# Stationary operands of 48 instead of 64 columns in the state products of a linear-attention and feed-forward kernel

## The chip, the cores and the metric

The kernel runs on one core of a Trainium2 chip. The metric is the device time of one execution in microseconds (us); lower is better. The engines are named as in the profile: PE is the matrix engine (PEld its weight loads, which overlap the products), DVE the vector engine, ACT the scalar engine, POOL the GpSimd engine, SP the queue that issues the DMA transfers.

## The reference, cut to what matters

```python
for t in range(S):                       # B, H, S, D = 4, 8, 768, 48
    kt, vt, rt = k[:, :, t], v[:, :, t], r[:, :, t]
    cur = einsum('bhd,bhe->bhde', u[None] * kt, vt)
    y[:, :, t] = einsum('bhd,bhde->bhe', rt, state + cur)
    state = w[None, :, :, None] * state + einsum('bhd,bhe->bhde', kt, vt)
x = y.transpose(0, 2, 1, 3).reshape(B * S, H * D)      # 3072 x 384
h = x @ w_in                                            # 384 x 2048
g = where(h > 0, h, exp(min(h, 0)) - 1)
out = g @ w_out                                         # 2048 x 384
```

## The kernel before, in words

The 768 tokens of a batch are cut into six blocks of 128 (n = 0 to 5). A pair of a block and one of the four batches is called a unit here, (n, b). The attention part works on units; the feed-forward part works on a whole block of four units, in 16 steps f = 0 to 15, one for each 128 columns of the hidden layer. A step holds nine wide products into `ps_h` (`hidden`, L1202), the activation, and nine wide products into `ps_acc` (`project`, L1258, of an earlier step). Beside the feed-forward steps of block n run the attention units of block n + 1, one unit for four steps. So units (1, b) run beside steps of block 0, and the later ones beside blocks 1 to 4. Beside block 0 the feed-forward weights are also made ready: each step, DVE joins words in `merge` and `sign` (L592, L600, into `wide`), ACT casts them in `split_w` (L620, into `wh`), and POOL takes the rest in `rest_w` (L630, into `wl`).

The engines take their instructions in the order in which the program issues them. That order is written out by hand: the string `FIRST` for steps of block 0 and `LATER` for the others. A word such as `ss9` names an operation and, in its last digit, the stage of a unit at which it is issued (8 is the unit's base step, 9 the step after it). In both strings the words of a step follow one another in program order, so a word that is moved is moved on the queue of its own engine.

A unit goes like this. `A` (`scores_halves`) computes the score products (L925) and behind them, in `added_halves` (L939), the products k by v that are added to the state, one for each head and each half of the block's 128 tokens: 16 products in a unit, 8 in units of the last block. Each counts as two weight loads and two matmuls in the trace. Their stationary operand is `k[HALVES[s], h, :]`, the head's 48 channels and 16 columns of padding, 64 columns; two heads share the 128 partitions of the result, which lies in the same PSUM banks as the scores. `pa` and `pb` (`take_halves`, L987, DVE) take the masked scores. `ss` (`sum_states`, DVE) adds the first half's products to the state, giving `mid` (L949), and the second half's to `mid`, giving `sw` (L952). `Y` (`outputs_halves`, L1003 and L1011) multiplies by the state, `mid` and the scores. `sw` (`next_state`, calling `decay_added`, L955, POOL) multiplies the tile `sw` by the decay and writes the state. The two words of a step that close the feed-forward's own work on DVE are `elu` (L1217) and `gl` (L1225), with `gh` (L1223) on ACT between them.

Of the kernel before, what the change touches and what calls it, by code (L numbers as in the profile page):

```python
# [8 lines left out]
F32 = mybir.dt.float32  # L9
# [8 lines left out]
P = 128  # L18
B, H, S, D = 4, 8, 768, 48
DP = 64  # L20
HP = H // 2
# [3 lines left out]
NCH = S // P  # L25
# [3 lines left out]
ROWS = [slice(i * DP, i * DP + D) for i in range(2)]  # L29
HALVES = [slice(i * DP, (i + 1) * DP) for i in range(2)]  # L30
# [18 lines left out]

FIRST = """  # L50

D9 lb ma ru4 hid wd Ya A9 neg rud8 t5 mb xya xaa sp elu ss9 kr8 kr4 pb9 bk7 rkb pa9 sum8 xha sum7 gh Lw xlda T8 dr8 gl br7 r3 r4 D7 m6 tka8 Gb swb vb proj
"""
LATER = """

A8 pb8 ss8 br7 rk9 hid pa8 neg rud4 kr4 xy9 Y8 elu t4 sw8 xa9 v9 bk6 gh gl xh9 xl9 G9 m4 proj D6 sum5
"""


class Kernel:  # L60
# [336 lines left out]
    def step(self, n, f):  # L397
        nc = self.nc

        k = f + 2 if n == 0 else NF + 1  # L400
        units = self.stages(n, f)


        last = divmod(n * NF + f - (1 if (n, f) < EARLY else 2), NF)
        both = {
            "ru": lambda n, b: self.current(n, b),
            "rud": lambda n, b: self.current(n, b, nc.vector),
            "sum": lambda n, b: self.current_sum(n, b),
            "kr": lambda n, b: self.key_rest(n, b),
            "krd": lambda n, b: self.key_rest(n, b, nc.vector),  # L410
            "D": lambda n, b: self.diag_halves(n, b),
            "A": lambda n, b: self.scores_halves(n, b),
            "pa": lambda n, b: self.take_halves(n, b, 0),
            "pb": lambda n, b: self.take_halves(n, b, 1),
            "ss": lambda n, b: self.sum_states(n, b),
            "Y": lambda n, b: self.outputs_halves(n, b),
            "xy": lambda n, b: self.take_outputs(n, b),
            "xa": lambda n, b: self.add_outputs(n, b),
            "sw": lambda n, b: self.next_state(n, b),
            "rk": lambda n, b: self.load_after(n, b, self.load_rk),  # L420
            "v": lambda n, b: self.load_after(n, b, self.load_v),
            "xh": lambda n, b: self.split_added(n, b, 0),
            "xl": lambda n, b: self.split_added(n, b, 1),
            "xld": lambda n, b: self.split_added(n, b, 1, nc.vector),
            "xhp": lambda n, b: self.split_added(n, b, 0, nc.gpsimd),
            "xhd": lambda n, b: self.split_added(n, b, 0, nc.vector),
            "xyd": lambda n, b: self.take_outputs(n, b, nc.vector.tensor_copy),
            "G": lambda n, b: self.fill_x(n, b),
        }
        by_pe = {  # L430
            "T": lambda n, b: self.turn_in(n, b),
            "dr": lambda n, b: self.decay_r(n, b),
            "dk": lambda n, b: self.decay_k(n, b),
            "tk": lambda n, b: self.take_k(n, b, nc.vector.tensor_copy),
            "tka": lambda n, b: self.take_k(n, b, nc.scalar.copy),
        }
        moved = {
            "t": lambda n, b: self.turn_blocks(n, b),
            "m": lambda n, b: self.move_blocks(n, b),
            "br": lambda n, b: self.decay_moved(n, b),  # L440
            "bk": lambda n, b: self.join_moved(n, b),
        }
        layer = {
            "hid": lambda: self.hidden(n, f, self.rest_of(n, f)),
            "ma": lambda: self.merge(k),
            "mb": lambda: self.sign(k),
            "neg": lambda: self.negative(n, f),
            "sp": lambda: self.split_w(k),
            "spd": lambda: self.split_w(k, nc.vector.tensor_copy),
            "r4": lambda: self.rest_w(k, 1),  # L450
            "r3": lambda: self.rest_w(k, 0),
            "r4d": lambda: self.rest_w(k, 1, nc.vector),
            "r3d": lambda: self.rest_w(k, 0, nc.vector),
            "elu": lambda: self.elu(n, f),
            "gh": lambda: self.split_g(n, f, 0),
            "gl": lambda: self.split_g(n, f, 1),
            "proj": lambda: self.project(*last) if last in self.g else None,
            "Lw": lambda: [self.load_weights(j) for j in (2 * k + 2 * DEEP - 1, 2 * k + 2 * DEEP) if n == 0],
            "wd": lambda: self.widen(k + 1),
            "lb": lambda: self.low_bits(k + 1),  # L460
        }
        for op in (LATER if n else FIRST).split():
            if op in layer:
                layer[op]()
                continue
            name, stage = op[:-1], int(op[-1], 16)
            for at, m, b in units:
                todo = {**both, **(by_pe if m == 1 else moved)}
                key = self.KINDS.get(name, name), m, b
                if at == stage and name in todo and key not in self.done:  # L470
                    self.done.add(key)
                    todo[name](m, b)
        if last[1] == NF - 1 and last[0] in self.acc:
            self.store(last[0])
        self.store_pending(2)
        if (n, f) == (0, NF - 1):

            o = self.late.bitcast(F32).rearrange("p s d w -> p (s d w)")[:, 0 : B * DM]
            self.o = o.rearrange("p (b d) -> p b d", b=B)
# [451 lines left out]
    def added_halves(self, n, b, banks):  # L931
        nc, un = self.nc, self.units[n, b]
        k, v = self.raw[n, b][1], self.v_of(n, b)
        un["kv"] = [t[:, 2 * P : 2 * P + HP * D] for t in banks]
        for a in range(HP):
            for i in range(2):
                for s in range(1 if n + 1 == NCH else 2):
                    h = 2 * a + i
                    nc.tensor.matmul(  # L939
                        un["kv"][s][HALVES[i], a * D : (a + 1) * D],  # L940
                        lhsT=k[HALVES[s], h, :], rhs=v[HALVES[s], h, :],
                        start=True, stop=True, skip_group_check=True,
                    )

    def sum_states(self, n, b):
        nc, un = self.nc, self.units[n, b]
        kv = [t.rearrange("p (a c) -> p a c", a=HP) for t in un["kv"]]
        mid = self.mid[:, :, 0:D]
        nc.vector.tensor_add(mid, self.state[b][:, :, 0:D], kv[0])  # L949
        if n + 1 < NCH:  # L950
            un["sw"] = self.wk.tile([P, HP, D], F32, tag="sw", name="sw", bufs=1)
            nc.vector.tensor_add(un["sw"], mid, kv[1])  # L952

    def decay_added(self, b, t):
        self.nc.gpsimd.tensor_mul(  # L955
            self.state[b][:, :, 0:D], t, self.pw[:, :, P : P + 1].to_broadcast([P, HP, D])
        )

    def next_state(self, n, b):
        if n + 1 < NCH:  # L960
            self.decay_added(b, self.units[n, b]["sw"])

    def first_state(self, b):
        nc = self.nc
# [373 lines left out]
```

## Time and profile before

| what | us |
|---|---|
| time, median of 3 runs | 491.83 (491.37 to 492.10) |
| span of the profiled execution, first to last instruction | 490.3 |
| around the span (median less span) | 1.5 |
| PE busy in the span | 479.5 (98%) |
| weight loads busy | 396.6 (81%) |
| DVE busy | 286.2 (58%) |
| ACT busy | 253.4 (52%) |
| POOL busy | 151.6 (31%) |

The profile comes from one execution, of which the span is what is recorded; the time of a run holds some 1.5 us more than it. Busy times are sums over stages that differ: beside block 0 (about 37 to 105 us from the start of the span) all four engines are nearly full, and later PE alone is.

### The profile page before, as it was taken

How to read it: one execution, taken by the hardware profiler on the slowest of the kernel's cores; microseconds unless marked ns; L12 is line 12 of the kernel's file. 1: busy time of each engine (PE TensorE's matmuls, PEld its weight loads, DVE VectorE, ACT ScalarE, POOL GpSimd, SP SyncE). 2: the span in 40 equal slices, each digit the busy share in tenths (PEclk: the TensorE clock that was granted, in tenths of full speed). 3: DMA queues.
4: the chain of work that ended last, by engine and by line, in shares of the span. 5: the costliest groups of instructions: out<-in, count | busy, mean ns of one | idle time of the engine just before them, and what ended most of it. 6: DMA issues, size and time to landing. Idle time of an engine off the chain costs nothing.

```text
span 490.3 us, 11493 instructions
## 1 busy us (share of the span) xinstructions
PE 479.5 (98%) x4640; PEld 396.6 (81%) x4640; DVE 286.2 (58%) x507; ACT 253.4 (52%) x453; POOL 151.6 (31%) x169
## 2 busy tenths in 40 slices
PE   8989999999999999999999999999999999999995
PEld 6788877878788888788888888888888888899994
DVE  8989999987555545745455565364554433433332
ACT  3469898864463443453553544544534535444442
POOL 5376769672241331241232223213203201000000
PEclk9999999999999999999999999999999999999999
DMA  7985866652543451443541623623524400020002
GB/s 160 227 202 172 195 181 191 158 130 70 124 128 84 117 138 43 122 123 73 141 114 38 153 86 84 157 59 96 146 58 123 108 13 11 18 48 0 1 0 71
DMA packets 109955, 51.04 MB, mean 104 GB/s; under 512 B 89027, under 2 KB 105797, under 8 KB 109893
## 3 DMA queue, kind: packets, MB, share of 16 engines
q1 hardware_dynamic: 109892, 50.22, 40.8%
q8 instruction: 38, 0.62, 0.6%
q14 instruction: 25, 0.20, 0.1%
HBM read 35.13 MB, written 13.11 MB: 98 GB/s over the span
## 4 chain that ended last, share of the span: by engine, by line
PE 81%; DVE 6%; POOL 3%; DMA 3%; SPq 2%; ACT 2%; issue 1%; DVEq 0%; ACTq 0%; POOLq 0%
PE ps_h L1202 36%; PE ps_acc L1258 29%; PE ps_acc L1245 7%; PE ps_y L1003 2%; DMA k_t<-in_k_dram 2%; PE ps_a L925 2%; POOL wl L630 2%; DVE wide L600 2%; DVE wide L592 2%; PE ps_y L1011 2%; PE ps_a L939 2%; DMA stage<-in_moe_w_out_dram 1%; SPq L205 1%; PE ps_y L873 1%; ACT wh L620 1%
## 5 line engine op out<-in xcount | busy, mean ns | idle before, releaser
L1202 PE MATMUL ps_h<-x,wh 128*128 128x512 f32 (+1 forms) x588 | 176.2, 389 | 0.0
L1258 PE MATMUL ps_acc<-g,wh 128*128 128x512 f32 x480 | 164.0, 396 | 0.0
L1217 DVE SCALAR_TENSOR_TENSOR ps_h<-g,ps_h 128x512 f32<-128x512 f32 x96 | 66.6, 693 | 145.5 <-ACT g L1212 145.5
L1211 ACT ACTIVATE g<-ps_h 128x512 f32<-128x512 f32 x96 | 57.3, 597 | 150.1 <-PE ps_h L1202 150.0
L1202 PEld LDWEIGHTS ps_h<-x,wh 128*128 128x128 f32 x588 | 108.2, 188 | 21.4
L1202 PE MATMUL ps_h<-x,wl 128*128 128x512 f32 (+1 forms) x294 | 109.0, 387 | 0.3
L1258 PEld LDWEIGHTS ps_acc<-g,wh 128*128 128x128 f32 x480 | 90.1, 188 | 20.2 <-DVE stage L1266 0.5
L1258 PE MATMUL ps_acc<-g,wl 128*128 128x512 f32 x240 | 93.6, 390 | 0.0
L1225 DVE TENSOR_TENSOR g<-ps_h,g 128x512 fp32r<-128x512 f32 x96 | 65.7, 685 | 42.6 <-ACT g L1223 40.6
L1223 ACT CAST g<-ps_h 128x512 fp32r<-128x512 f32 x96 | 56.2, 585 | 43.4 <-DVE ps_h L1217 43.2
L1202 PEld LDWEIGHTS ps_h<-x,wl 128*128 128x128 f32 x294 | 55.0, 188 | 12.6 <-POOL wl L630 1.6
L1212 ACT ACTIVATE g<-g 128x512 f32<-128x512 f32 x96 | 60.7, 632 | 3.1
L1040 POOL TENSOR_TENSOR x<-x_f,x 128x512 fp32r<-128x512 f32 x16 | 20.7, 1292 | 116.3 <-ACT x L1038 116.3
L753 POOL TENSOR_TENSOR k_t<-k_t,rev 128x384 f32<-128x384 f32 x21 | 23.7, 1133 | 100.6 <-DVE ru L735 100.4
L1258 PEld LDWEIGHTS ps_acc<-g,wl 128*128 128x128 f32 x240 | 45.1, 188 | 8.4
L630 POOL TENSOR_TENSOR wl<-wide,wh 128x384 fp32r<-128x384 f32 x29 | 33.8, 1190 | 15.9 <-ACT wh L620 15.9
L1245 PE MATMUL ps_acc<-wh,g 128*128 128x384 f32 x128 | 35.1, 337 | 0.0
L980 POOL TENSOR_TENSOR a<-ident_h,diag 128x512 f32<-128x512 f32 x20 | 23.7, 1185 | 2.5 <-PE ps_a L925 2.5
L1245 PEld LDWEIGHTS ps_acc<-wh,g 128*128 128x128 f32 x128 | 23.4, 188 | 0.6
L600 DVE SCALAR_TENSOR_TENSOR wide<-stage,wide 128x768 int32<-128x768 int32 (+1 forms) x17 | 21.3, 1256 | 0.5
L1245 PE MATMUL ps_acc<-wl,g 128*128 128x384 f32 x64 | 21.5, 336 | 0.0
L674 POOL TENSOR_TENSOR rk<-rk,pw 128x512 f32<-128x512 f32 x16 | 19.0, 1190 | 5.7 <-DMA rk<-blocks 5.7
(128 smaller groups left out, 460.3 us busy)
## 6 DMA issues: line engine op xcount, KB each, us to landing
blocks<-tb SPq DMA_DIRECT2D x64, 128.0 KB
rk<-blocks SPq DMA_DIRECT2D x16, 512.0 KB
stage<-in_moe_w_out_dram SPq DMA_DIRECT2D x16, 384.0 KB
stage<-in_moe_w_in_dram SPq DMA_DIRECT2D x32, 144.0 KB
r_t<-in_r_dram SPq DMA_DIRECT2D x22, 192.0 KB
k_t<-in_k_dram SPq DMA_DIRECT2D x22, 192.0 KB
v_t<-in_v_dram SPq DMA_DIRECT2D x22, 192.0 KB
out_dram<-stage SPq DMA_DIRECT2D x80, 48.0 KB
```

The source lines that it names most:

```text
L600: self.nc.vector.scalar_tensor_tensor(a, high, -(2**31), a, op0=ALU.bitwise_and, op1=ALU.bitwise_or)
L630: (eng or self.nc.gpsimd).tensor_sub(lo, a, hi.bitcast(F32))
L753: (eng or self.nc.gpsimd).tensor_mul(k, k, self.rev[:, :, 0:D])
L980: self.nc.gpsimd.tensor_mul(un["a"], self.ident_h.unsqueeze(1).to_broadcast([P, H, DP]), un["diag"].unsqueeze(2).to_broadcast([P, H, DP]),)
L1202: self.nc.tensor.matmul(ph[:, part], lhsT=a[:, c * P : (c + 1) * P], rhs=x[:, c, part], start=(i == 0), stop=(i + 1 == len(todo)),)
L1211: nc.scalar.activation(g, ph, AF.Relu, scale=-1.0)
L1212: nc.scalar.activation(g, g, AF.Exp, scale=-1.0)
L1217: self.nc.vector.scalar_tensor_tensor(ph, g, -1.0, ph, op0=ALU.add, op1=ALU.max)
L1223: nc.scalar.copy(part, g)
L1225: nc.vector.tensor_sub(part, g, self.g[n, f][2].bitcast(F32))
L1245: self.nc.tensor.matmul(self.acc[n][b][:, 0:DM], lhsT=a[:, at], rhs=w, start=(f == 0 and i == 0), stop=(f == NF - 1 and i == 2),)
L1258: self.nc.tensor.matmul(self.acc[n][c], lhsT=w[:, c * P : (c + 1) * P], rhs=g, start=(f == 0 and i == 0), stop=(f == NF - 1 and i == 2),)
```

## The change

In `added_halves` the stationary operand loses its padding: `k[HALVES[s], h, 0:D]`, 48 columns, and the result lies on `ROWS[i]`, partitions 0 to 47 and 64 to 111, instead of all 128. Since 16 partitions between the two ranges are no longer written, everything that read the sums in one instruction over 128 partitions now goes by two ranges of 48. `sum_states` writes only `mid`, in two instructions. What made `sw` is now a part of its own. Beside block 0 it is `se` (`sum_ends`): two DVE additions. Later it is `ta` (`take_ends`), two ACT copies out of PSUM, and `ad` (`add_ends`), two POOL additions of `mid`. `next_state` calls `decay_rows`, two POOL multiplications. In `FIRST`, `ss9` moves from behind `elu` to ahead of it and `se9` comes behind `pb9`; in `LATER`, `ta8 ad8` come behind `pa8`, ahead of `neg`.

```diff
-... sp elu ss9 kr8 kr4 pb9 bk7 rkb pa9 ...            (FIRST)
+... sp ss9 elu kr8 kr4 pb9 se9 bk7 rkb pa9 ...
-A8 pb8 ss8 br7 rk9 hid pa8 neg rud4 ...                (LATER)
+A8 pb8 ss8 br7 rk9 hid pa8 ta8 ad8 neg rud4 ...
...
-                        un["kv"][s][HALVES[i], a * D : (a + 1) * D],
-                        lhsT=k[HALVES[s], h, :], rhs=v[HALVES[s], h, :],
+                        un["kv"][s][ROWS[i], a * D : (a + 1) * D],
+                        lhsT=k[HALVES[s], h, 0:D], rhs=v[HALVES[s], h, :],
...
     def sum_states(self, n, b):
+        un = self.units[n, b]
+        for rows in ROWS:
+            kv = un["kv"][0][rows].rearrange("p (a c) -> p a c", a=HP)
+            self.nc.vector.tensor_add(self.mid[rows, :, 0:D], self.state[b][rows, :, 0:D], kv)
+
+    def sum_ends(self, n, b):
...
+        for rows in ROWS:
+            kv = un["kv"][1][rows].rearrange("p (a c) -> p a c", a=HP)
+            self.nc.vector.tensor_add(un["sw"][rows], self.mid[rows, :, 0:D], kv)
+
+    def take_ends(self, n, b):
...
+        for rows in ROWS:
+            kv = un["kv"][1][rows].rearrange("p (a c) -> p a c", a=HP)
+            self.nc.scalar.copy(un["sw"][rows], kv)
+
+    def add_ends(self, n, b):
...
+        for rows in ROWS:
+            self.nc.gpsimd.tensor_add(un["sw"][rows], un["sw"][rows], self.mid[rows, :, 0:D])
...
+    def decay_rows(self, b, t):
+        for rows in ROWS:
+            self.nc.gpsimd.tensor_mul(
+                self.state[b][rows, :, 0:D], t[rows],
+                self.pw[rows, :, P : P + 1].to_broadcast([D, HP, D]),
+            )
 
     def next_state(self, n, b):
         if n + 1 < NCH:
-            self.decay_added(b, self.units[n, b]["sw"])
+            self.decay_rows(b, self.units[n, b]["sw"])
```

## Rows read from the trace of the kernel before

**Rows 1.** Two stretches: us, then busy us (instructions) of PE, PEld, DVE, ACT, POOL.
```profile
77.00:97.00 20.00, 19.85 (x208) 15.86 (x207) 18.52 (x26) 17.83 (x33) 15.96 (x13) 1.00 0.62 172
200.00:300.00 100.00, 100.00 (x1033) 81.05 (x1034) 53.17 (x102) 46.81 (x86) 26.29 (x27) 1.00 0.43 107
```

**Rows 2.** The chain that ended last, 92 to 140 us: start, us, what.
```profile
96.04 1.19 POOL state L955
...
101.02 2.67 POOL wl L630 x2
...
103.74 0.96 PE ps_h L1202 x3
...
113.44 2.27 PE ps_h L1202 x9
```

**Rows 3.** DVE in order of time, 78.5 to 88.5 us: start, duration, what.
```profile
79.79 1.67 DVE L600 SCALAR_TENSOR_TENSOR wide<-stage,wide 128x768 int32<-128x768 int32 x1
81.38 0.68 DVE L1217 SCALAR_TENSOR_TENSOR ps_h<-g,ps_h 128x512 f32<-128x512 f32 x1
81.98 0.34 DVE L949 TENSOR_TENSOR mid<-state,ps_a 128x192 f32<-128x192 f32 x1
82.45 0.35 DVE L952 TENSOR_TENSOR sw<-mid,ps_a 128x192 f32<-128x192 f32 x1
82.72 0.77 DVE L987 COPY_PREDICATED a<-mask,ps_a 128x256 f32<-128x256 int32 x2
83.39 0.68 DVE L1225 TENSOR_TENSOR g<-ps_h,g 128x512 fp32r<-128x512 f32 x1
83.99 1.13 DVE L592 SCALAR_TENSOR_TENSOR wide<-stage 128x768 int32<-128x768 int32 x1
85.15 1.65 DVE L600 SCALAR_TENSOR_TENSOR wide<-stage,wide 128x768 int32<-128x768 int32 x1
```

**Rows 4.** ACT in order of time, 78.5 to 88.5 us, with idle time ahead.
```profile
81.50 0.93 ACT L620 CAST wh<-wide 128x384 fp32r<-128x384 f32 x2 [0.26 <-DVE wide L600]
82.33 0.58 ACT L1223 CAST g<-ps_h 128x512 fp32r<-128x512 f32 x1
...
86.83 0.93 ACT L620 CAST wh<-wide 128x384 fp32r<-128x384 f32 x2 [0.62 <-DVE wide L600]
```

**Rows 5.** Weight loads in order of time, at 23 to 26 and at 262 us.
```profile
23.63 0.55 PEld L968 LDWEIGHTS ps_st<-raw 128*64 128x64 f32 x16
24.73 0.97 PEld L776 LDWEIGHTS ps_a<-rk 48*128 48x128 f32 x16 [0.55 <-DVE x L894]
...
262.35 0.56 PEld L939 LDWEIGHTS ps_a<-v_t,k_t 64*64 64x64 f32 x32
```

**Rows 6.** Groups of instructions over the whole span: busy us, mean ns of one load.
```profile
L939 PEld LDWEIGHTS ps_a<-v_t,k_t 64*64 64x64 f32 x576 | 11.2, 135 | 0.0
...
L776 PEld LDWEIGHTS ps_a<-rk 48*128 48x128 f32 x64 | 3.9, 187 | 1.9 <-POOL rk L696 0.8 <-DVE x L894 0.5 <-DVE rk L698 0.4
```

**Rows 7.** The instructions of line 955: count, duration min/median/max in ns.
```profile
L955 POOL TENSOR_TENSOR state<-sw,pw x16: 514/518/1227, 55.3 to 323.6; 128x192 f32<-128x192 f32 x16
```

**Rows 8.** DVE in order of time, 92 to 106 us: the transpose that waits.
```profile
101.05 0.71 DVE L651 STREAM_TRANSPOSE tb<-k_t 128x512 f32<-128x512 f32 x1 [0.30 <-POOL k_t L753]
```

**Rows 9.** DVE in order of time, 41 to 46.5 us: L600 beside an idle POOL.
```profile
44.96 0.96 DVE L600 SCALAR_TENSOR_TENSOR wide<-stage,wide 128x768 int32<-128x768 int32 x1
```

**Rows 10.** A unit beside block 2, engines in order of time, 261.9 to 275 us.
```profile
264.19 0.44 DVE L987 COPY_PREDICATED a<-mask,ps_a 128x256 f32<-128x256 int32 x1
...
267.87 0.67 DVE L651 STREAM_TRANSPOSE tb<-k_t 128x512 f32<-128x512 f32 x1
...
265.34 0.60 ACT L1211 ACTIVATE g<-ps_h 128x512 f32<-128x512 f32 x1 [2.77 <-PE ps_h L1202]
...
265.74 1.02 POOL L753 TENSOR_TENSOR k_t<-k_t,rev 128x384 f32<-128x384 f32 x1 [7.29 <-DVE ru L735]
...
265.23 0.46 PE L1003 MATMUL ps_y<-rk,state 48*64 48x64 f32 x16
```

More of the change, by code (lines that the diff above doesn't have):

```diff
@@ L50 @@
 FIRST = """
-D9 lb ma ru4 hid wd Ya A9 neg rud8 t5 mb xya xaa sp elu ss9 kr8 kr4 pb9 bk7 rkb pa9 sum8 xha sum7 gh Lw xlda T8 dr8 gl br7 r3 r4 D7 m6 tka8 Gb swb vb proj
+D9 lb ma ru4 hid wd Ya A9 neg rud8 t5 mb xya xaa sp ss9 elu kr8 kr4 pb9 se9 bk7 rkb pa9 sum8 xha sum7 gh Lw xlda T8 dr8 gl br7 r3 r4 D7 m6 tka8 Gb swb vb proj
 """
 LATER = """
-A8 pb8 ss8 br7 rk9 hid pa8 neg rud4 kr4 xy9 Y8 elu t4 sw8 xa9 v9 bk6 gh gl xh9 xl9 G9 m4 proj D6 sum5
+A8 pb8 ss8 br7 rk9 hid pa8 ta8 ad8 neg rud4 kr4 xy9 Y8 elu t4 sw8 xa9 v9 bk6 gh gl xh9 xl9 G9 m4 proj D6 sum5
 """
@@ L415, in step @@
             "ss": lambda n, b: self.sum_states(n, b),
+            "se": lambda n, b: self.sum_ends(n, b),
+            "ta": lambda n, b: self.take_ends(n, b),
+            "ad": lambda n, b: self.add_ends(n, b),
             "Y": lambda n, b: self.outputs_halves(n, b),
@@ L945, in sum_states @@
     def sum_states(self, n, b):
[L946 to L952, printed above, removed]
+        un = self.units[n, b]
[3 more added lines that the diff above has]
+    def sum_ends(self, n, b):
+        un = self.units[n, b]
+        if n + 1 == NCH:
+            return
+        un["sw"] = self.wk.tile([P, HP, D], F32, tag="sw", name="sw", bufs=1)
+        for rows in ROWS:
+            kv = un["kv"][1][rows].rearrange("p (a c) -> p a c", a=HP)
+            self.nc.vector.tensor_add(un["sw"][rows], self.mid[rows, :, 0:D], kv)
+    def take_ends(self, n, b):
+        un = self.units[n, b]
+        if n + 1 == NCH:
+            return
+        un["sw"] = self.wk.tile([P, HP, D], F32, tag="sw", name="sw", bufs=1)
+        for rows in ROWS:
+            kv = un["kv"][1][rows].rearrange("p (a c) -> p a c", a=HP)
+            self.nc.scalar.copy(un["sw"][rows], kv)
+    def add_ends(self, n, b):
+        un = self.units[n, b]
+        if n + 1 == NCH:
+            return
+        for rows in ROWS:
+            self.nc.gpsimd.tensor_add(un["sw"][rows], un["sw"][rows], self.mid[rows, :, 0:D])
     def decay_added(self, b, t):
```

## The prediction, made before the changed kernel ran

> **What bounds the kernel now.** I read the busy times by stretch first, because the change does different things in two stages. In a stretch of 100 us in the middle PE is busy all of it, DVE about half, POOL a quarter [rows 1]: there PE's own work alone sets the time, and whatever makes its products shorter comes off the end. Beside block 0 it is another picture: in 20 us, PE 19.85, DVE 18.52, ACT 17.83, POOL 15.96 [rows 1]. When four engines are that full, the question is which loop of waits sets the pace. The chain shows PE released by POOL there, at 103.74 us, by the rest of a weight (L630), with the decay of the state (L955) earlier on that chain [rows 2]. So PE is not what bounds it. Nor is POOL, if one asks what starts its rests: the casts on ACT (L620), which start when DVE's L600 ends [rows 4].
>
> The loop itself is read from DVE and ACT side by side. In a step without a unit's sums it goes L600, L620 on ACT, L1223 on ACT, then DVE again. In the step that holds them it is DVE alone: L600 at 79.79, L1217, L949, L952, two L987, L1225 at 83.39, L592, and the next L600 at 85.15, with hardly a gap [rows 3]; the ACT cast that L1225 needs ended at 82.91, 0.48 us before it was wanted, and ACT then waited 0.62 us for that next L600 [rows 4]. One such step stands here for each of the four units (1, b). An instruction put between L600 and L1225 there is on the loop.
>
> **The products.** How much does a load of 48 columns save? I saw no row of one at this clock. In L939, 32 loads take 0.56 us over four tiles of the array [rows 5]; less one load's own 0.135 [rows 6], 31 intervals, 13.7 ns each, 55 ns for a round of four. In L968, two tiles, 16 loads take 0.55 [rows 5]: 27.5 ns each, again 55 ns for a round. So the pace is a tile's, not that of issue. L776 loads 128 columns into two tiles: 0.97 [rows 5] less 0.19 [rows 6] over 15 intervals, 104 ns a round. From 64 to 128 columns a round thus grows by 0.77 ns a column; 48 would take 43, 12 ns less. The moving operand has 48 columns already, so I don't expect it to hold the round up. A unit with 16 products has eight rounds, of which the first loads under the tail of the scores: seven times 12 is 0.086 us; a last-block unit, three times, 0.037. Beside blocks 1 to 4 stand twelve of the former and four of the latter: 1.2 us off PE's saturated stretch. From below: nothing, if a load pays for the tile's 64 columns whatever is in it. From above, all rounds count: 1.35. I take 1.2, as the rounds follow the column count. In the four units (1, b) a shorter product gains nothing, as PE waits there.
>
> **The DVE additions beside block 0.** Two become four, each over the same 192 elements of a partition. I read no row with 48 partitions; half as many partitions cost as much, or some part of it down to nothing, and I take the whole, since the stream of 192 elements is what stays. From start to start, L952 to L987 is 0.27 us [rows 3], so two more add 0.55 between L600 and L1225; 0.94 if each takes the 0.47 that lies between L949 and L952. Moving the first two ahead of `elu` delays the ACT cast L1223 by about as much, which its 0.48 and the later additions on DVE hide. Behind L1225 all is late by 0.55: L592, L600, the casts, the rests on POOL, PE's next product. Four units: 2.2 us.
>
> **The POOL decay beside block 0.** One L955 becomes two; it takes 0.51 at the least and 1.23 at the most [rows 7]. Behind it on POOL are the products that prepare the next k, then the rests that PE waits for [rows 2]. For the steps of (1, 1) and (1, 2), POOL's lateness runs beside DVE's and the larger counts. Ahead of (1, 3) it adds: there DVE's transpose already waited 0.30 us for POOL's k [rows 8], so DVE gets later by what POOL gets later. I take 0.5, between nothing and 1.23: the long L955 started while an L600 of 1.65 or so ran, against 0.96 for one beside an idle POOL [rows 3, 9], and the second half comes when that is over. The Trainium skill (SBUF — State Buffer, Who interferes with whom) has a rule for this: a DVE instruction with two SBUF inputs and a GpSimd one that reads SBUF exclude each other for a whole instruction. By that rule the second half costs 0.5; by doubling the longest row 1.2, and the forecast would be 0.7 higher.
>
> **The later blocks' new work.** DVE keeps two additions. ACT gets two copies of 192 elements, at most 0.58 each by L1223 with 512 [rows 4], ahead of an activation that waits 2.77 us for PE [rows 10]: hidden; without that cover up to 1.2 a unit. POOL gets two additions and one more decay, 0.5 to 1.2 each by L955 [rows 7]. It idles 7.29 us up to L753, which has to be done only for the transpose at 267.87, 1.1 us after its end [rows 10]. Additions that get in the way of the DVE products for which L753 waits may push it by 1.0 and still fit. Next to be late would be the transfer for the following unit, not PE. The outputs on PE at 265.23 need the scores taken, which is done at 264.63 [rows 10], and now ACT's copies too, since both lie in the banks that the outputs reuse: L939's loads end at 262.91 [rows 5], two copies by 264.1. Cost: nothing.
>
> **Sum.** 2.2 and 0.5, less 1.2: 1.5 us. The profiled span of 490.3 becomes 491.8; around it the runs have 1.5 more, so 491.83 becomes 493.3, slower by 0.3%. About 0.2%, 1 us, is what a measurement of this kernel tells from no change.
>
> **Rivals.** *The loads don't shrink:* a tile of 64 columns keeps its 55 ns. Against it, rounds of 64 and 128 columns differ nearly in proportion [rows 5]. Then 491.83 + 2.7 = 494.5. *The additions are absorbed*, which ends on the other side. DVE's L592 and L600 took 1.13 and 1.65 beside POOL's rests, and L600 0.96 beside an idle POOL [rows 3, 9]. Shifted by half a microsecond against POOL, they may stop colliding: up to 0.7 back for each L600, more than the 0.55 spent. With nothing lost beside block 0 the time is 490.6; it is faster than before once block 0 costs under 1.2 us, 0.3 a unit. For it: every long L600 was one beside POOL. Against it: POOL's own queue moves too. *Half absorbed:* the collision is undone in one or two of the four steps, block 0 costs 1.2 to 1.6, and the time stays at 491.8 to 492.2. *A later unit waits:* ACT's copies, run late, hold the banks and with them the outputs; it decides once they end after 265.23 in such a unit, 1.1 us later than they can. At 0.2 us a unit over twelve units this is 2.4 more: 495.7. The 2.77 us of idle ACT speak against it.
>
> **How the numbers follow.** The sum as it stands 0.48, no smaller loads 0.12, absorbed 0.18, half absorbed 0.18, a later wait 0.04. The first stays within 0.2% in a fifth of its cases (a unit costing 0.4 instead of 0.55), so slower 0.54, same 0.28, faster 0.18. Low is 490.6, all absorbed; high 494.8, just above loads that don't shrink; the likeliest case by itself spans 492.4 to 494.3.
>
> **What would show it.** L939's 32 loads in about 0.47 instead of 0.56 us, and a unit's period beside block 2 shorter by 0.09. Beside block 0, four additions where two were, and from L600 to L600 in that step 5.9 instead of 5.36; L955 as pairs with a second half near 0.5; PE's first wide product of block 1, now at 113.44 [rows 2], later by 2.7. The prediction is wrong if that product is not at least 1.5 us late, if L939 keeps 0.56, or if PE shows gaps ahead of the outputs from block 1 on.

## The result, and the profile after

The changed kernel takes 495.11 us (median of 4 runs, 494.8 to 496.3); the kernel before, on the same chip, 491.78 (4 runs, 491.37 to 492.1). The ratio is 1.007, 95% interval 1.0057 to 1.0082: slower by 3.3 us, where the forecast was slower by 1.5, in a range that ended at 494.8. The profiled execution has a span of 494.6 us and is the run of 496.3; its mean granted clock was 0.993. The other three runs had 0.996 to 0.999 and took 494.8 to 495.35. The changed kernel was run a second time as an experiment (e11, below), and that profile, with a clock of 0.999, is the cleaner one for sums.

The later blocks first, since there the forecast held. These are the stretches of [rows 1], the columns as there.

```profile
77.00:97.00 20.00, 18.97 (x205) 15.15 (x204) 18.52 (x27) 17.36 (x31) 15.82 (x15) 1.00 0.67 174
200.00:300.00 100.00, 100.00 (x1027) 81.11 (x1026) 56.59 (x107) 51.40 (x98) 37.01 (x42) 1.00 0.44 109
```

From 200 to 300 us PE is still busy all the time. DVE has 3.4 us more, ACT 4.6 and POOL 10.7, and none of it delays PE. Beside block 0 (the first stretch) PE lost 0.88 us of its 20, and DVE is as full as it was. The weight loads of the state products, in order of time, answer to [rows 5]:

```profile
267.27 0.47 PEld L942 LDWEIGHTS ps_a<-v_t,k_t 64*48 64x48 f32 x32
```

Next, instructions by line: count, duration min/median/max in ns. The first answers to [rows 6], the second to [rows 7].

```profile
L942 PEld LDWEIGHTS ps_a<-v_t,k_t x576: 116/122/122, 38.1 to 399.6; 64*48 64x48 f32 x192
...
L986 POOL TENSOR_TENSOR state<-sw,pw x32: 503/512/1223, 55.9 to 329.3; 48x192 f32<-48x192 f32 x32
```

32 loads take 0.47 instead of 0.56 us, one load 122 ns (median) instead of a mean of 135. The decay comes in pairs, and a half costs 0.51 us in the median, as the whole did.

DVE in order of time, in the step that holds the sums of unit (1, 1), and at the transpose ahead of unit (1, 3) [rows 3, 8]:

```profile
59.86 1.67 DVE L603 SCALAR_TENSOR_TENSOR wide<-stage,wide 128x768 int32<-128x768 int32 x1
61.45 0.72 DVE L952 TENSOR_TENSOR mid<-state,ps_a 48x192 f32<-48x192 f32 x2
62.20 0.69 DVE L1249 SCALAR_TENSOR_TENSOR ps_h<-g,ps_h 128x512 f32<-128x512 f32 x1
62.93 0.45 DVE L1019 COPY_PREDICATED a<-mask,ps_a 128x256 f32<-128x256 int32 x1
63.28 0.72 DVE L961 TENSOR_TENSOR sw<-mid,ps_a 48x192 f32<-48x192 f32 x2
64.03 0.45 DVE L1019 COPY_PREDICATED a<-mask,ps_a 128x256 f32<-128x256 int32 x1
64.37 0.68 DVE L1257 TENSOR_TENSOR g<-ps_h,g 128x512 fp32r<-128x512 f32 x1
64.97 1.19 DVE L595 SCALAR_TENSOR_TENSOR wide<-stage 128x768 int32<-128x768 int32 x1
66.19 1.66 DVE L603 SCALAR_TENSOR_TENSOR wide<-stage,wide 128x768 int32<-128x768 int32 x1
...
104.07 0.71 DVE L654 STREAM_TRANSPOSE tb<-k_t 128x512 f32<-128x512 f32 x1 [1.39 <-POOL k_t L756]
```

From L603 (L600 before) to the next L603 there are 6.33 us where [rows 3] had 5.36: 0.97 more, of which 0.75 is the two more additions (1.44 for four, 0.69 for two). The taking of the scores, now in two rows, is 0.90 instead of 0.77. L595 and L603 (L592 and L600 before) took 1.19 and 1.66, nearly as before (1.13 and 1.65). The transpose waits 1.39 us for POOL's k instead of 0.30. POOL in order of time, in the same step and beside block 2:

```profile
55.93 1.81 POOL L986 TENSOR_TENSOR state<-sw,pw 48x192 f32<-48x192 f32 x2
57.82 1.02 POOL L737 TENSOR_TENSOR ru<-r_t,u_b 128x384 f32<-128x384 f32 x1
58.91 1.79 POOL L738 TENSOR_TENSOR ru<-ru,k_t 128x384 f32<-128x384 f32 x1
60.78 1.63 POOL L756 TENSOR_TENSOR k_t<-k_t,rev 128x384 f32<-128x384 f32 x1
62.38 4.65 POOL L633 TENSOR_TENSOR wl<-wide,wh 128x384 fp32r<-128x384 f32 x4
...
268.99 1.57 POOL L977 TENSOR_TENSOR sw<-sw,mid 48x192 f32<-48x192 f32 x2 [5.56 <-ACT sw L970]
271.11 1.03 POOL L756 TENSOR_TENSOR k_t<-k_t,rev 128x384 f32<-128x384 f32 x1 [0.55 <-POOL sw L977]
```

The decay pair takes 1.81 us, and behind it L738 takes 1.79 though it has the work of L737, which took 1.02. So the rests (L633) begin 2.52 us after L603 and end at 67.03. What that does to DVE is the subject of the experiments.

PE in order of time, at the end of block 0 and at the first wide product of block 1:

```profile
104.19 1.52 PE L1234 MATMUL ps_h<-x,wh 128*128 128x512 f32 x6
106.74 0.96 PE L1234 MATMUL ps_h<-x,wl 128*128 128x512 f32 x3 [1.03 <-POOL wl L633]
108.45 0.94 PE L1035 MATMUL ps_y<-rk,state 48*64 48x64 f32 x14 [0.74 <-DVE sw L961]
...
118.78 0.73 PE L1234 MATMUL ps_h<-x,wh 128*128 128x512 f32 x2
...
270.06 0.46 PE L1035 MATMUL ps_y<-rk,state 48*64 48x64 f32 x16
```

PE stands still twice in unit (1, 3): for the rest of a weight, and then for the additions of the state. The first wide product of block 1 is at 118.78 instead of 113.44 [rows 2]. The chain that ended last, 100 to 125 us, goes back from those outputs over DVE to POOL's k:

```profile
103.01 1.03 POOL k_t L756
...
104.07 0.71 DVE tb L654
...
108.83 0.98 PE ps_y L1035 x26
```

In a later unit ACT's two copies come in time, which answers to [rows 10]; the last row is one of DVE in the same unit:

```profile
268.60 0.65 ACT L970 COPY sw<-ps_a 48x192 f32<-48x192 f32 x2 [1.11 <-DVE a L1019]
...
...
270.14 0.83 DVE L738 TENSOR_TENSOR ru<-ru,k_t 128x384 f32<-128x384 f32 x1
```

They end at 269.25, 0.8 us before the outputs at 270.06. The activation that had waited 2.77 us for PE still waits 0.91. DVE's product in the last row reads the k that POOL's L756 then overwrites; beside POOL's additions it takes 0.83 us where it took 0.56.

### The profile page after: what moved, and what is told of

The parts are those of the page before. It is cut to its first block, busy times and chain, and to the rows that moved or that the text cites. A ratio compares the mean times of both kernels' runs of the same rounds, so it can differ in the third digit from the quotient of the medians.

```text
span 494.6 us, 11609 instructions
## 1 busy us (share of the span) xinstructions
PE 479.1 (97%) x4640; PEld 395.9 (80%) x4640; DVE 294.8 (60%) x519; ACT 261.5 (53%) x477; POOL 178.3 (36%) x209
## 4 chain that ended last, share of the span: by engine, by line
PE 78%; DVE 9%; POOL 5%; DMA 3%; issue 2%; ACT 2%; SPq 1%; DVEq 0%; POOLq 0%
PE ps_h L1234 34%; PE ps_acc L1290 29%; PE ps_acc L1277 7%; DVE wide L603 3%; PE ps_y L1035 2%; DVE wide L595 2%; PE ps_a L928 2%; PE ps_y L1043 2%; DMA stage<-in_moe_w_in_dram 2%; POOL a L1012 1%; POOL state L986 1%; PE ps_a L942 1%; POOL wl L633 1%; ACT wh L623 1%; POOL ru L737 1%
## 5 line engine op out<-in xcount | busy, mean ns | idle before, releaser
L977 POOL TENSOR_TENSOR sw<-sw,mid 48x192 f32<-48x192 f32 x24 | 18.2, 759 | 58.4 <-ACT sw L970 57.5
L633 POOL TENSOR_TENSOR wl<-wide,wh 128x384 fp32r<-128x384 f32 x29 | 32.3, 1140 | 18.5 <-ACT wh L623 18.5
L756 POOL TENSOR_TENSOR k_t<-k_t,rev 128x384 f32<-128x384 f32 x21 | 23.2, 1107 | 29.7 <-DVE ru L738 23.4
L603 DVE SCALAR_TENSOR_TENSOR wide<-stage,wide 128x768 int32<-128x768 int32 (+1 forms) x17 | 21.3, 1255 | 0.5
```

The costliest lines, as they stand in the source:

```text
L603: self.nc.vector.scalar_tensor_tensor(a, high, -(2**31), a, op0=ALU.bitwise_and, op1=ALU.bitwise_or)
L633: (eng or self.nc.gpsimd).tensor_sub(lo, a, hi.bitcast(F32))
L756: (eng or self.nc.gpsimd).tensor_mul(k, k, self.rev[:, :, 0:D])
```

## The experiments

Ten kernels ran; each ratio below is against runs of the kernel before taken beside it. In the expectations the theories have letters. **A**: the two more additions lie on DVE's loop, each at its price. **B**: the decay in two halves makes POOL late. **C**: the new places of the additions cost. **D**: the later blocks' new work costs. After four runs two more were formed, **L** (what counts is only that POOL is late by half a microsecond, so that instructions collide) and **M** (the halves' own reads are in the way); after those, **J** (a unit's loop grows by the additions' time, less what the joinings L592 and L600 save by starting later).

**e1, later units only.** The units (1, b) are as before; all others as in the changed kernel.

```diff
-    lhsT=k[HALVES[s], h, :],
+    lhsT=k[HALVES[s], h, 0:D] if n > 1 else k[HALVES[s], h, :],
...
+    if n == 1:
...
-    self.decay_added(b, self.units[n, b]["sw"])
+    (self.decay_added if n == 1 else self.decay_rows)(b, self.units[n, b]["sw"])
```

> The units beside block 0 keep everything of the kernel before (64 stationary columns, sums and decay over 128 partitions, the order in FIRST); the later units have the change. Theory A (all the loss arises beside block 0, PE's shorter products are a clean gain later): block 1 starts at the same time as before, 113.4 us, a unit's period in the later blocks is about 0.09 shorter, and the time is 1.1 us (0.2%) under the kernel before. Rival D (the later blocks' new ACT and POOL work costs something there): gain under 0.5 us, and PE gaps ahead of the outputs in the later blocks.

490.33 us (6 runs, 490.1 to 490.86) against 491.73, ratio 0.997, interval 0.9958 to 0.9982. This is faster than both kernels, by 1.4 us against the one before. Its chain from 105 to 116 us is PE alone; here is the first wide product of block 1:

```profile
113.21 2.26 PE ps_h L1242 x9
```

Five units from 242 us on take 94.28 us from scores to scores, 94.78 before: 0.10 a unit. D falls; the narrower loads are worth what the forecast gave them.

**e2, first units only.** The mirror image: narrow products, four additions and two decays in the units (1, b), the rest as before.

> Only the units beside block 0 have the change, with its order in FIRST; the later units are as before. Theory A: block 1 starts 4 us late or more, as in the changed kernel, and nothing is regained: 4 to 5.5 us over the kernel before, the upper end where TensorE's granted clock falls to half once beside block 0. Rival D: not more than the changed kernel's 3.3.

497.44 us (5 runs, 496.04 to 498.0) against 491.73, ratio 1.0113, interval 1.0097 to 1.0129. The later units are as they were, so the whole loss is beside block 0. The median lies 5.7 us above the kernel before, a little over the 5.5 that was expected. Two of its runs, at mean clocks of 0.998 and 0.999, took 496.04 and 496.26; the three others, at 0.995 and 0.996, 497.44 to 498.0. The loss of the first two, 4.4, less e1's gain of 1.4 is about the loss of the whole change.

**e3, the additions alone.** The kernel before, with products as they were; in the units (1, b) each of the two additions goes by two halves of 64 partitions, in the old place.

```diff
...
+    for half in HALVES:
+        nc.vector.tensor_add(self.mid[half, :, 0:D], self.state[b][half, :, 0:D], kv[0][half])
+    for half in HALVES:
+        nc.vector.tensor_add(un["sw"][half], self.mid[half, :, 0:D], kv[1][half])
```

> The kernel before, with one edit: beside block 0 the two DVE additions of a unit are four, each over one half of the 128 partitions, at the old place behind the activation. Products, decay and order stay. Theory A (the additions are on the loop of DVE and ACT that sets the pace there): about 0.7 us for each of three units and as much or more for the fourth, 2 to 3.5 us over the kernel before; from L600 to L600 in such a step about 6.1 instead of 5.36. Theory B (the POOL decay in two parts, which holds up the next k and the weights' rests, makes most of the loss): under 1 us. Theory C (the moved order is what costs): under 1 us.

494.03 us (5 runs, 493.56 to 495.23) against 491.73, ratio 1.0041, interval 1.0028 to 1.0055.

**e4, the decay alone.** The kernel before, with POOL's decay of the units (1, b) in two halves of 64 partitions.

```diff
...
+    for half in HALVES:
+        self.nc.gpsimd.tensor_mul(
+            self.state[b][half, :, 0:D], sw[half],
+            self.pw[half, :, P : P + 1].to_broadcast([DP, HP, D]))
```

> The kernel before, with one edit: beside block 0 the POOL decay of a unit's state is two instructions, each over one half of the partitions. Theory A: POOL's lateness is hidden in the first units and shows only ahead of the fourth: 0 to 0.8 us over the kernel before. Theory B: 2 us or more. Theory C: under 1 us.

494.46 us (5 runs, 494.23 to 494.91) against 491.73, ratio 1.0056, interval 1.0043 to 1.007. POOL's one more instruction a unit costs no less than DVE's two (the two intervals overlap), although it is the shorter work.

How can that be? The loop of DVE, from the start of L600 in the step with the sums of unit (1, 1) to that with those of (1, 2), tells it. The rows are windows of the instructions that write `wide` (the joinings L592 and L600, eight in a loop): length, DVE busy with them. First the kernel before, then the changed one, e3 and e4.

```profile
59.43:79.79 20.36, 10.79 (x9) 1.00 0.68 186
```
```profile
59.86:80.98 21.12, 10.64 (x9) 1.00 0.68 177
```
```profile
61.51:82.12 20.61, 10.28 (x9) 1.00 0.71 183
```
```profile
59.01:80.11 21.10, 11.18 (x8) 1.00 0.67 180
```

In e3 the additions take 1.45 us instead of 0.69, but the joinings give 0.51 back, and the loop is longer by 0.25. In e4 no addition is added, but the joinings take 0.39 more, 0.35 more passes outside them, of which 0.24 lies ahead of one L592, and the loop is longer by 0.74. With both, as in the changed kernel, nearly all of the joinings' saving is gone (0.15 left), and the loop is longer by 0.76. The two costs don't add here: the additions delay L592 and L600 past POOL's rests, and the late decay moves the rests after them. The instructions behind it, DVE in e3:

```profile
63.69 0.72 DVE L951 TENSOR_TENSOR mid<-state,ps_a 64x192 f32<-64x192 f32 x2
64.45 0.73 DVE L953 TENSOR_TENSOR sw<-mid,ps_a 64x192 f32<-64x192 f32 x2
...
66.47 1.32 DVE L592 SCALAR_TENSOR_TENSOR wide<-stage 128x768 int32<-128x768 int32 x1
67.83 0.96 DVE L600 SCALAR_TENSOR_TENSOR wide<-stage,wide 128x768 int32<-128x768 int32 x1
```

and DVE in e4:

```profile
58.02 0.95 DVE L592 SCALAR_TENSOR_TENSOR wide<-stage 128x768 int32<-128x768 int32 x1
...
63.55 1.75 DVE L592 SCALAR_TENSOR_TENSOR wide<-stage 128x768 int32<-128x768 int32 x1 [0.17 <-POOL wl L630]
65.33 1.65 DVE L600 SCALAR_TENSOR_TENSOR wide<-stage,wide 128x768 int32<-128x768 int32 x1
```

and POOL, in the kernel before and then in e4:

```profile
55.29 1.22 POOL L955 TENSOR_TENSOR state<-sw,pw 128x192 f32<-128x192 f32 x1
...
58.66 1.62 POOL L753 TENSOR_TENSOR k_t<-k_t,rev 128x384 f32<-128x384 f32 x1
60.23 5.39 POOL L630 TENSOR_TENSOR wl<-wide,wh 128x384 fp32r<-128x384 f32 x4
```
```profile
55.08 1.81 POOL L966 TENSOR_TENSOR state<-sw,pw 64x192 f32<-64x192 f32 x2
...
58.07 1.78 POOL L735 TENSOR_TENSOR ru<-ru,k_t 128x384 f32<-128x384 f32 x1
...
61.52 4.64 POOL L630 TENSOR_TENSOR wl<-wide,wh 128x384 fp32r<-128x384 f32 x4
```

Before, the four rests begin 0.80 us after L600 and end at 65.62, so the second L600, issued at 64.79, stands for some 0.7 us behind the last of them: 1.65 with its own work. In e3 DVE comes later, L592 is the one that meets the last rest, and L600 runs alone in 0.96. In e4 DVE's L592 (58.02) and POOL's L735 (58.07) begin within 0.05 us of each other, and POOL's takes 1.78 instead of 1.01; with the decay's second half the rests begin 2.51 us after L600. Both L592 and L600 then stand behind a rest, at 1.75 and 1.65. Ahead of that L592 its row names a wait of 0.17 us for a rest: it writes a place in `wide` that POOL must have read, so this part is a wait for data.

The Trainium skill (SBUF — State Buffer, Who interferes with whom) says that a DVE instruction with two SBUF inputs contends with a GpSimd instruction that reads SBUF, that the ports they share are an exclusive lock, and that the order of issue decides which of the two blocks. These rows agree: 0.96 for an L600 alone and 1.65 to 1.75 for joinings that stood behind a POOL instruction of 1.0.

The same account, from the first score products of each unit in PE's order of time (the last column ends at those of unit (2, 0)), in us, from one profiled execution each:

| kernel | (1, 0) to (1, 1) | to (1, 2) | to (1, 3) | to (2, 0) |
|---|---|---|---|---|
| before | 20.28 | 20.36 | 20.37 | 13.44 |
| e1, block 0 as before | 20.27 | 20.34 | 20.37 | 13.45 |
| e3, additions in two | not comparable | 20.60 | 20.62 | 14.26 |
| e4, decay in two | 20.31 | 21.11 | 21.10 | 14.31 |
| e9, POOL late (below) | 20.31 | 20.82 | 20.83 | 13.90 |
| e11, all of the change | 21.08 | 21.08 | 21.12 | 15.29 |

(In e3's profiled execution ACT waited 1.91 us for a weight's transfer at 39.91, in the first column.) The decay of unit (1, 0) runs at 55 us, shortly ahead of the end of the first column, and split alone (e4) it adds 0.03 there. So the 0.8 there is the additions. In the middle the change costs what the decay costs alone; in the last column the two add, 0.82 and 0.87 alone and 1.85 together. PE's waits in unit (1, 3) say why: in e4 it waits once, 0.95 us for a rest, in e3 once, 0.75 us for DVE, and in the changed kernel for both in turn.

**e8, the moved words alone.** The kernel before with the order of the changed one, all sums over 128 partitions.

```diff
-... sp elu ss9 kr8 kr4 pb9 bk7 ...
+... sp ss9 elu kr8 kr4 pb9 se9 bk7 ...
```

> The kernel before with the order of the changed one beside block 0 and nothing else: the first addition of a unit stands ahead of the activation, the second behind the first taking of scores; each is one instruction over 128 partitions, and products and decay are as before. Theory C (the order is what costs): 1 us or more over the kernel before. Theories A and L: within 0.5 us of it.

491.42 us (11 runs, 491.11 to 492.69) against 491.57, ratio 0.9999, interval 0.999 to 1.0007. C falls.

**e9, POOL late without the halves.** The kernel before, and on POOL behind each decay of the units (1, b) two memsets of a tile that nothing reads; so it does work that the reference doesn't ask for.

```diff
+    if n == 1:
+        late = self.wk.tile([P, 160], F32, tag="late_by", name="late_by")
+        for _ in range(2):
+            self.nc.gpsimd.memset(late, 0.0)
```

> The kernel before with two POOL memsets of 128x160 (about 0.5 us together) into a tile that nobody reads, behind each unit's decay beside block 0. They add lateness on POOL and no reads. Theory L (lateness by half a microsecond is what turns into collisions on DVE): 2 to 3 us over the kernel before, like the decay in two parts. Rival M (the second half of the decay itself gets in DVE's way where it stands, by its reads): under 1 us.

492.99 us (10 runs, 492.64 to 493.22) against 491.57, ratio 1.0027, interval 1.0018 to 1.0036: 1.4 us, between what L and M expected. The two memsets took 0.52 us, as long as half a decay, and POOL's products behind them kept their 1.01. The loop from (1, 1) to (1, 2) grew by 0.46, all of it in the joinings (11.26 us). So lateness alone gives 1.4 of e4's 2.7 us. The other 0.28 us a unit is no joining time, which is as long in e4 (11.18), but the 0.35 that passes outside the joinings in e4 and does not here. The rows show what differs: here L735 begins ahead of L592, and L592 is the one that stands; in e4 L592 began 0.05 us ahead, and L735 stood.

```profile
57.94 1.01 POOL L735 TENSOR_TENSOR ru<-ru,k_t 128x384 f32<-128x384 f32 x1
...
58.12 1.64 DVE L592 SCALAR_TENSOR_TENSOR wide<-stage 128x768 int32<-128x768 int32 x1
```

So in e4 the rests are later still, and L592 waits for one. That this order makes up all of the difference is read from the rows and was not tried.

**e7 and e6, the decay one step earlier.** In the changed kernel (e7) and in e1 (e6), the word that issues the decay in `FIRST` goes from stage b to stage a, a step earlier.

```diff
-... tka8 Gb swb vb proj          (FIRST)
+... tka8 Gb swa vb proj
```

> The changed kernel whole, with one word of FIRST moved: the decay of a unit's state beside block 0 is issued one step earlier, right behind the outputs that read the state, where POOL idles some 2.4 us, instead of ahead of the products for the next k. Theory L (two additions move DVE out of POOL's way, half a microsecond more of POOL in front moves POOL back into it; the loss is the collision): without the late POOL the additions cost 0.25 us a unit as they did alone, and the time falls by 2 us or more, to 491 to 493. Theory A (the additions on DVE's loop alone make the loss, whatever POOL does): it stays at 494.5 to 495.5.

> Beside block 0 the products and sums of the kernel before, with the decay issued one step earlier; the later units have the change. Theory L: POOL's rests come up to 1.2 us earlier than in the kernel before, ahead of DVE's joining of words, so the unit's period beside block 0 shrinks too, and the time falls below the 490.3 of the later units' change alone: 487 to 489.5. Theory A: 490.3 as before the move, since DVE's own work is unchanged.

e7: 495.92 us (6 runs, 494.26 to 496.81) against 491.57, ratio 1.008, interval 1.0064 to 1.0096. e6: 491.26 (11 runs, 490.6 to 491.67), ratio 0.9988, interval 0.9978 to 0.9998, so 0.9 slower than e1 had been. Both miss what L expected, and both lie 0.4 to 1 us above what A did. In e7 the same loop is 21.28 us long with 10.80 in the joinings: they are back at their length of before, and the additions are paid in full. The decay stood earlier on POOL, and the collisions were no fewer. L, as a recipe, falls: that POOL is late matters only by which joinings then meet which POOL instructions.

**e10, six additions.** As e3, but the second sum in four quarters of 32 partitions.

```diff
...
+    for i in range(4):
+        q = slice(32 * i, 32 * i + 32)
+        nc.vector.tensor_add(un["sw"][q], self.mid[q, :, 0:D], kv[1][q])
```

> The kernel before, with one edit: beside block 0 a unit's two DVE additions are six, two halves of the partitions for the first and four quarters for the second, at the old place. Theory J (DVE's loop sets the pace, and what the additions cost there is their own time less the time that they save the two joinings behind them, which stand blocked while POOL's last rests run; with six additions both joinings come after the rests): 1.45 us more of additions and about 0.85 less of joining for each unit, so a period of some 21.0 instead of 20.36, and 2.5 to 3.5 us over the kernel before. Theory A (each addition is simply added to the loop at its 0.36): a period of 21.8, and 5 us or more.

The loop came out as J had it. The window of the joinings and DVE behind the additions:

```profile
61.87:82.91 21.04, 9.92 (x9) 1.00 0.68 180
```
```profile
67.60 0.95 DVE L592 SCALAR_TENSOR_TENSOR wide<-stage 128x768 int32<-128x768 int32 x1
68.59 0.96 DVE L600 SCALAR_TENSOR_TENSOR wide<-stage,wide 128x768 int32<-128x768 int32 x1
```

The additions take 2.23 us, 1.54 more than before; the joinings save 0.87, since now both run alone. That 20.36 grows to 21.04 is 0.68 for twice as many more additions as in e3, which cost 0.25. But the time, 497.55 us (4 runs, 496.06 to 498.57) against 491.43, ratio 1.0112, interval 1.0097 to 1.0127, is 6.1 more, and J had expected far less. In this profiled execution the first column of the table above is 23.33 and the last 16.58, and the granted clock fell in both. Its fastest run, 496.06 at a mean clock of 0.998, is still 4.6 more. J holds for the loop and misses the time; A's time, 5 us or more, came, but not its loop of 21.8. What the rest of the 6.1 is was not settled.

**e11, the changed kernel again**, for its spread and a second profile.

> The changed kernel once more, for a second profile of the last stretch beside block 0. If the fall of TensorE's granted clock to half belongs to the change, it shows in this execution too; if it is met by chance after the two gaps that PE has there, an execution without it gives a span some 1.5 us shorter, 493.0 to 493.2, with the same gaps.

494.8 us (6 runs, 494.3 to 498.47) against 491.43, ratio 1.0086, interval 1.0063 to 1.0109. The profiled execution took 494.3, span 492.6, clock 0.999; the span is 0.4 below what was expected of an execution without the fall, and its first scores of unit (1, 0) come 0.45 sooner than in the first profile. PE in order of time, at the end of block 0 as above:

```profile
106.29 0.96 PE L1234 MATMUL ps_h<-x,wl 128*128 128x512 f32 x3 [1.04 <-POOL wl L633]
107.99 0.78 PE L1035 MATMUL ps_y<-rk,state 48*64 48x64 f32 x14 [0.74 <-DVE sw L961]
...
116.81 0.73 PE L1234 MATMUL ps_h<-x,wh 128*128 128x512 f32 x2
```

PE's waits are the same as in the first profile, 1.04 and 0.74 us. But from the outputs to the first wide product there are 8.82 us, and in the first profile 10.33. The difference is the clock: from 108 to 112 us (us, busy of PE, PEld, DVE, ACT, POOL, then the granted clock), first the changed kernel's first profile, then e11's.

```profile
108.00:112.00 4.00, 3.50 (x67) 3.08 (x68) 2.76 (x8) 2.03 (x5) 0.62 (x1) 0.61 0.25 68
```
```profile
108.00:112.00 4.00, 3.95 (x75) 3.30 (x76) 3.16 (x8) 2.40 (x6) 1.18 (x2) 1.00 0.44 136
```

## Why the prediction was off

**The products: right.** Loads of 48 columns in 0.47 us and 0.10 us a unit were forecast as 0.47 and 0.09. e1, which has this gain alone, is 1.4 us faster; the term was 1.2. The rival in which the loads don't shrink falls.

**The later blocks: right.** ACT's copies end 0.8 us before the outputs need the banks, where 1.1 was reckoned. From block 1 on PE waited for them once, 0.18 us ahead of the outputs of unit (2, 0), in both profiles of the changed kernel. That is the gap that the prediction named as a sign of being wrong. e1, with the same later units, has none: the chain goes from that wait over ACT's copies to POOL's decay in halves. L756 begins 0.14 us behind DVE's L738, which POOL's additions slowed, and ends 0.55 us before the transpose that needs it, where it was 1.1 (the forecast allowed 1.0 of delay), without PE waiting.

**The additions beside block 0: total near, price and mechanism off.** Four of them are in the loop, as foreseen. One more costs 0.36 to 0.39 us, not the 0.27 that the forecast read from L952 to L987. The step "two more add 0.55 between L600 and L1225" should have been 0.75, which lies inside the bounds given, 0 to 0.94. By themselves (e3) they get 0.5 of it back in the middle units, as the rival "absorbed" had it: L600 escapes a rest. So by the table e3's four units come to some 2.1 (0.8 of e11's first column, where the decay adds 0.03; then 0.24, 0.25 and 0.82), against 2.2 forecast as four times 0.55. That the totals agree is luck: a price too low, and a saving left out.

**The POOL decay: the step that failed.** The prediction took POOL off the loop: "Nor is POOL, if one asks what starts its rests: the casts on ACT (L620)". That holds for the pairs of rests that wait for a cast. The four in the step with the sums begin without a wait where POOL's own L753 ends (60.23 in the kernel before), and e9, which only makes POOL late by 0.52 us, costs 0.46 a unit. From that premise it said: "For the steps of (1, 1) and (1, 2), POOL's lateness runs beside DVE's and the larger counts", and ahead of (1, 3) "I take 0.5". The rule came out in form: in the middle units the change costs what its larger part costs, and ahead of (2, 0) the two add. But the larger part is POOL's, 0.75, where the forecast had DVE's 0.55; DVE's alone is 0.25. The second half itself did cost 0.51, but it was treated as a delay that is handed on at its own length. By the table e4 costs 0.75, 0.73 and 0.87, altogether 2.35 (and 0.03 in the first column), where the forecast had 0.5 for the last alone and nothing of its own for the others. Half a microsecond on POOL makes L735 collide with L592, which makes the rests late by 1.7 against DVE, which makes L592 and L600 stand behind them.

**The sum.** Beside block 0, without a fall of the clock, e11's four columns are 0.80, 0.72, 0.75 and 1.85 longer, 4.1 in all; forecast 2.7. Behind it the spans end 1.24 us nearer to those scores (492.6 − 115.83 against 490.3 − 112.29). The first scores of unit (1, 0) come 0.58 sooner in e11, which the change doesn't touch. 4.1 − 1.2 − 0.6 is the 2.3 by which the spans differ. The median of the runs is higher by 3.3, in part because of which executions were profiled: the one before was, by its span, the slowest of its four runs (492.1), e11's the fastest of its six. The forecast also had no term for the clock: in the changed kernel's first profile it fell at the end of block 0, and the column to (2, 0) took 16.78 instead of 15.29, 1.5 us more. Of the changed kernel's ten runs seven took 494.3 to 495.35, at mean clocks of 0.996 to 0.999, and three 496.17 to 498.47, at 0.991 to 0.993. So a fall lengthens some runs, and the greater part of the 3.3 is there without one.

**The tests that it named.** From L600 to L600 6.33 us, forecast 5.9; the first wide product of block 1 later by 3.4 in e11 and 5.3 in the first profile, forecast 2.7; L939's loads, the unit's period and the halves of the decay as forecast. The sign came as forecast: "absorbed" was true in part, of the additions alone in the middle units, and the decay undid it. That the decay undoes it is shown by e3, e4 and the changed kernel side by side. The exact order of collisions in each of the other steps was read from single rows and not tried.

## What to carry to other kernels

Where two engines hold each other up instruction by instruction, cost an added instruction by where it moves the others, not by its own length: here, in the two middle units, 0.5 us more on POOL cost 0.75 each, and 0.76 us more on DVE cost 0.25. And two such costs need not add (there they didn't, in the last unit they did), so each should be measured alone and together. A change that shortens work in one stage and lengthens it in another can be made in the one only: with the new products in the later units alone (e1) the kernel takes 490.33 us and beats both.

## What the runs showed that was not expected

- These instructions are no cheaper over fewer partitions. The median of DVE's additions of 192 elements is between 344 and 354 ns over 128, 64, 48 or 32 partitions, that of POOL's decay between 512 and 518 over 128, 64 or 48. The forecast assumed the whole price, with nothing as its lower bound; that held at every size that ran.
- The same waits of PE can be followed by a fall of the clock or not. In the changed kernel's two profiles PE waited 1.03 and 0.74 us, and 1.04 and 0.74, at the end of block 0. In the first the granted clock behind them was 0.50 for 3.41 us from 108.9 on, that is 1.2 of 2.4 GHz, and in the second it stayed at 1.00. The same work took 1.5 us longer in the first.
